# Chunk 0's second row loads through SyncE's queue behind a hold, the weights wait for it, and one key product moves to VectorE

## The chip, the cores and the metric

The kernel runs on one core of a Trainium2 chip. The core has five engines that take their instructions in order, each from its own list: TensorE (PE, matrix products; its loads of stationary operands are shown as PEld), VectorE (DVE), ScalarE (ACT), GpSimd (POOL) and SyncE (SP, which here only issues transfers). Sixteen DMA engines move data between the chip's memory and the core's on-chip memory; a transfer is issued by an engine, POOL or SP for nearly all of them, and lands later. The metric is the device time of one execution in microseconds, as the median of several runs.

## The reference: a gated linear recurrence, then a bilinear feed-forward layer

For 4 batches, 8 heads, 768 tokens and head size 48, the first part keeps a state of 48x48 per batch and head. Each token scales the state's rows by its own alpha, adds the outer product of its key and value, and reads the state with its query:

```python
for t in range(S):
    state = alpha[:, :, t, :, None] * state + np.einsum('bhd,bhe->bhde', k[:, :, t], v[:, :, t])
    y[:, :, t] = np.einsum('bhd,bhde->bhe', q[:, :, t], state)
```

The second part takes all 3072 tokens with their 8x48=384 numbers as x, and gives `(x @ w_a) * (x @ w_b) @ w_out`, with w_a and w_b of 384x1536 and w_out of 1536x384. All inputs and the output are float32.

## The kernel before: six chunks, and a program written out by hand

The work is cut into six chunks, 0 to 5. A chunk holds 256 tokens of two batches; chunks 0 and 1 are the first 256 tokens of batches 0-1 and 2-3, chunks 2 and 3 the next 256, and so on. The two batches of a chunk are its rows, 0 and 1 (in the program, a first argument 0 or 1; `a` and `b` behind it are the two halves of the heads, and `*` is both rows). Two neighbouring tokens share one of the 128 partitions, so a tile of q, k or alpha is 128 x 2 rows x 8 heads x 2 tokens x 48.

A chunk runs through these steps. `ld` loads alpha, q, k or v. `ln` takes the logarithm of alpha on ScalarE. `B`/`Bs` (chunk 0) or `H`, `L`, `A2` (chunk 1) make the running sums of the logarithms over the tokens with a triangular matrix on TensorE, and `E` takes the exponential of a sum or of its negative. `lv` first brings the first of two neighbouring tokens to the level of the second: keys times alpha, queries times the exponential of minus the logarithm (`level`, one multiplication in place on the tile of k or q). `mk` and `mq` multiply keys and queries by the exponentials and write them as bf16 into QKp (`mul`). `C` transposes QKp on TensorE, `Ce` copies the result; `K` and `k` make the new state; `D` makes the scores, `M` or `Mc` with `Mm` mask them; `SB`, `SA` and `Y` add up the outputs, and `X` copies them into xT. The feed-forward part then works on pieces of 128 of the 1536 columns: `a` and `b` are the products with w_a and w_b, `as` copies one of them, `pr` multiplies the two, `o` is the product with w_out, `ot` copies it out and `st` stores it.

The order is written out in the string PROGRAM: each line names a chunk and its steps, and every step appends its instructions to the lists of its engines at once. A step's last letter gives the engine where there is a choice: V for VectorE, P for GpSimd, S for ScalarE, Y for SyncE. So the order of PROGRAM is the order on each engine, and nothing reorders it later. Waits between engines are put in by the framework, from which tile an instruction reads or overwrites. Tiles of alpha, q and k have two buffers each, so chunk 2's alpha goes into chunk 0's buffer and chunk 3's into chunk 1's, and such a load waits for the last instruction that reads the old contents. Loads on POOL's queue also wait so that at most eight are under way.

Around the change: chunk 0's row 0 is loaded in six pieces by SP (`ld a 0b Y` and the like); row 1's alpha, q and k, v, all weights (`W`, `Wo`, which also turn them from float32 into bf16) and chunk 1's loads are issued by POOL. `W b 0 256` loads columns 0 to 255 of w_b. Between its issues POOL builds the constants: `cs` and `cz` clear tiles, `cm` builds half a mask, `c2` and `c3` convert the triangular matrix. A step `gate` exists: POOL copies one element of a tile into a small tile `go`, and so waits until it is there; before the change it is used once in another form (`gatet`), late in the kernel. For row 1 of chunk 1, `lv 1 k P` and `lv 1 q P` stand on POOL with `ld a * P` of chunk 3 between them, and `lv 0 k V` of row 0 on VectorE.

Lines: the loads are line 411, the weights 391, the logarithms 418, `Bs` 465, `lv` 524, `mk` and `mq` 550, `Ce` 599 (VectorE), the transposes 591, the state update 660 and 661, the masks 677 and 685, `pr` 798, the products with w_a and w_b 784 and with w_out 806, and the copy of a gate 858.

Of the kernel before, what the change touches and what calls it, by code (L numbers as in the profile page):

```python
# [14 lines left out]


PROGRAM = """
0: c1a; c1; fill 7 2; cz 0 q V; cz 0 b P; cs 0 m P; ci; cz 1 q V; cz 0 v V; ld a 0b Y; ln 0b; cs 0 0 P; cm 0; cu; cu2 P; B 0b 3; Bs 0b; cs 1 m P; ld v 0 P; ld a 1 P
0: cz 1 b P; ld a 0a Y; ln 0a; B 0a 1; Bs 0a; E 0a b; fill 9 2; cus; ld q 0a Y; mq 0a V; E 0b i; ld q 0b Y; ld k 0a Y; ld k 0b Y; mk 0b V; E 0b b; mq 0b V
0: C 0 1 5; E 0a i; mk 0a V; Ce 0 1 V; C 0 0 3; Ce 0 0 V; dk 0 6; fill 1 1; v 0 S; de 0; K 0 0 7; k 0 0 V; ln 1; cs 1 0 P; ld q 1 P; ld k 1 P; W b 0 256  # L20
0: cm 1; ld v 1 P; c2 P; c3 P; D 0 1 5; M 0 1; D 0 0 0; SB 0 6; B 1a 4; Bs 1a; Mc 0 0; Mm 0 0 V; B 1b 5; Bs 1b; E 1a i; E 1a b; mq 1a V; mk 1a V; K 0 1 4; E 1b i
0: v 1 V; mk 1b V; E 1b b; mq 1b V; SA 0; Y 0; X 0 S; dk 1 0; C 1 0 3; Ce 1 0 V; k 0 1 V; b 1 0 6; W a 0 256; de 1; K 1 0 5; k 1 0 V
1: ld a 1 P
0: W a 256 768; W b 256 768
# [35 lines left out]
0: b 0 1 6  # L60
1: Ce 0 1 S
2: ld k * P
1: lv 1 k P
3: ld a * P
0: pr 0 1
1: mk 1 V; lv 1 q P; mq 1 V
# [202 lines left out]
def kernel(  # L269
# [11 lines left out]
    nc = tc.nc  # L281
    B, H, S, D = q.shape
    assert (B, H, S, D) == (4, 8, 768, 48)
    C = 128
# [14 lines left out]
    ld = ctx.enter_context(tc.tile_pool(name="ld", bufs=2))  # L299
# [89 lines left out]
    def load_w(w, lo, hi):  # L389
        src, dst = ((moe_w_a, wa_t), (moe_w_b, wb_t))[w]  # L390
        nc.gpsimd.dma_start(out=dst[:, :, lo:hi], in_=src[:, lo:hi].rearrange("(t p) f -> p t f", p=128))  # L391

    def load_o(lo, hi):
        nc.gpsimd.dma_start(out=wo_t[:, lo:hi, :], in_=moe_w_out[lo * 128:hi * 128, :].rearrange("(k p) f -> p k f", p=128))
# [11 lines left out]
    def load(ch, what, us, eng):  # L406
        if not hasattr(ch, what):
            setattr(ch, what, ld.tile([C, 2, H, 2, D], BF16 if what == "v" else F32, name=what + "_t", bufs=3 if what == "v" else 2))
        t, src = getattr(ch, what), {"a": alpha, "k": k, "q": q, "v": v}[what]
        us, hs = us  # L410
        eng.dma_start(out=t[:, us, hs].rearrange("p b h r d -> p (b h) (r d)"),  # L411
                      in_=src[ch.b0 + us.start:ch.b0 + us.stop, hs, ch.s * 2 * C:(ch.s + 1) * 2 * C, :].rearrange("b h (p r) d -> p (b h) (r d)", r=2))

    def logs(ch, us):
        if not hasattr(ch, "la"):
            ch.la = wk.tile([C, 2, H, 2, D], F32, name="la", bufs=1)
        us, hs = us
        nc.scalar.activation(out=ch.la[:, us, hs].rearrange("p b h r d -> p (b h r d)"), in_=ch.a[:, us, hs].rearrange("p b h r d -> p (b h r d)"), func=AF.Ln)  # L418

    def pairs(ch, us, eng):  # L420
        if not hasattr(ch, "l2"):
            ch.l2 = wk.tile([C, 3, H, D], F32, name="l2", bufs=1)
        us, hs = us
        ch.apart -= set(range(us.start, us.stop))
        x = ch.la[:, us, hs].rearrange("p b h r d -> p (b h) r d")
        eng.tensor_add(ch.l2[:, us, hs].rearrange("p b h d -> p (b h) d"), x[:, :, 0, :], x[:, :, 1, :])
# [419 lines left out]
    def us(u):  # L846
        return ALL if u == "*" else ONE[int(u)]

    def uh(u):
        return us(u[0]), slice(0, H) if len(u) == 1 else slice(0, H // 2) if u[1] == "a" else slice(H // 2, H)  # L850
# [5 lines left out]
    def gate_t(x, u):  # L856
# [17 lines left out]
        "fill": lambda x, n, i: fill(int(n), i),  # L874
        "warm": lambda x, n, i: warm(int(n), i),
        "ld": lambda x, what, u, e: load(x, what, uh(u), ENG[e]),
        "W": lambda x, w, lo, hi: load_w("ab".index(w), int(lo), int(hi)),
        "Wo": lambda x, lo, hi: load_o(int(lo), int(hi)),
        "ln": lambda x, u: logs(x, uh(u)),
        "l2": lambda x, u, e: pairs(x, uh(u), ENG[e]),  # L880
        "A": lambda x, u, i: cum(x, uh(u), i),
# [81 lines left out]
```

## Time and profile before

| | us |
|---|---|
| median of 3 runs | 194.72 (194.59 to 195.71) |
| the profiled execution | 195.32 |
| its span, first to last instruction | 193.5 |
| PE busy | 184.7 (95% of the span) |
| DVE busy | 138.4 (71%) |
| ACT busy | 103.3 (53%) |
| POOL busy | 50.8 (26%) |
| granted clock of TensorE | 1.00 |

The profile is of one execution. Busy times are of instructions that compute; issuing a transfer is shown with its own rows, and the time from an issue to its landing apart from it. A wait names the engine or transfer whose end came last. In rows of the timeline the first number is the start in us from the span's start and the second the length; where several instructions are merged, xN is their count, and [x <- y] is the idle time ahead of it and what ended it. The 16 DMA engines can have several packets under way, so their share can be above 1.

### The profile page before, as it was taken

To read this page: it belongs to the slowest core of one execution; us is meant where nothing else is said; L and a number is where in the kernel's file an instruction comes from. 1 tells how busy PE (TensorE), PEld (TensorE's weight loads), DVE (VectorE), ACT (ScalarE), POOL (GpSimd) and SP (SyncE) were. 2 spreads that over 40 slices of the span, in tenths; PEclk is the share of its full clock that TensorE was granted. 3 is DMA by queue.
4 is the path that set the end of the run, shared out by engine and by line. 5 is a ranking of instruction groups with operands and counts; after the bars stand their busy time and mean duration, and the time that the engine had idled before them with its cause. 6 is when DMAs were issued, how large, how long until landed. Compare 5 with 4: busy or idle time off the path is not lost.

```text
span 193.5 us, 5877 instructions
## 1 busy us (share of the span) xinstructions
PE 184.7 (95%) x2509; PEld 111.4 (58%) x2509; DVE 138.4 (71%) x230; ACT 103.3 (53%) x189; POOL 50.8 (26%) x71
## 2 busy tenths in 40 slices
PE   7889699999999998999999999999999999999993
PEld 3467475666687865744556644555544566544462
DVE  4688777999899799597979499875854871156520
ACT  4565575886775676556565235875255622154401
POOL 8999645850640425000400020050000000000000
PEclk9999999999999999999999999999999999999999
DMA  5999999999999999489995488999297005021013
GB/s 139 261 214 211 243 247 251 252 246 260 243 220 231 198 234 219 57 233 213 172 219 69 100 203 178 118 191 120 59 180 160 3 3 122 0 99 67 0 42 122
DMA packets 67162, 30.96 MB, mean 160 GB/s; under 512 B 58064, under 2 KB 65120, under 8 KB 67136
## 3 DMA queue, kind: packets, MB, share of 16 engines
q0 software_dynamic: 18640, 14.16, 41.3%
q1 hardware_dynamic: 48352, 16.34, 39.9%
q8 instruction: 19, 0.31, 0.7%
q10 hardware_dynamic: 144, 0.10, 0.2%
q14 instruction: 7, 0.06, 0.1%
HBM read 25.98 MB, written 4.74 MB: 159 GB/s over the span
## 4 chain that ended last, share of the span: by engine, by line
PE 84%; POOL 6%; DMA 5%; issue 2%; DVE 1%; ACT 0%; POOLq 0%; DVEq 0%
PE psum L784 47%; PE psum L806 24%; DMA wb_t<-in_moe_w_b_dram 5%; PE psum L672 3%; PE psum L722 2%; PE psum L625 2%; PE psum L696 2%; PE psum L701 1%; PE psum L505 1%; PE psum L817 1%; POOL v_t L411 1%; POOL a_t L411 1%; PE psum L591 1%; POOL wa_t L391 1%; DVE prod L798 1%
## 5 line engine op out<-in xcount | busy, mean ns | idle before, releaser
L784 PE MATMUL psum<-xT,wb_t 128*128 128x512 bf16 (+1 forms) x270 | 57.0, 337 | 1.3 <-DMA wb_t<-in_moe_w_b_dram 1.3
L784 PE MATMUL psum<-xT,wa_t 128*128 128x512 bf16 (+1 forms) x270 | 56.1, 337 | 0.0
L806 PE MATMUL psum<-wo_t,prod 128*128 128x384 bf16 x276 | 48.5, 326 | 0.0
L784 PEld LDWEIGHTS <-wb_t 128*128 128x128 bf16 x270 | 25.5, 98 | 21.9 <-DMA wb_t<-in_moe_w_b_dram 1.6
L784 PEld LDWEIGHTS <-wa_t 128*128 128x128 bf16 x270 | 25.6, 98 | 19.7 <-issue 0.2
L806 PEld LDWEIGHTS <-prod 128*128 128x128 bf16 x276 | 26.1, 98 | 17.0
L681 ACT ACTIVATE m<-psum 128x1024 bf16<-128x1024 f32 x16 | 16.3, 1023 | 6.1 <-PE psum L672 5.9
L823 DVE COPY ot<-psum 128x384 f32<-128x384 f32 (+1 forms) x13 | 6.9, 538 | 15.7 <-PE psum L806 13.2
L524 POOL TENSOR_TENSOR q_t<-q_t,ra 128x384 f32<-128x384 f32 x8 | 8.8, 1103 | 34.7 <-DVE prod L798 18.4
L821 ACT ACTIVATE ot<-psum 128x384 f32<-128x384 f32 (+1 forms) x12 | 5.7, 477 | 12.9 <-PE psum L806 11.9
L524 POOL TENSOR_TENSOR k_t<-k_t,a_t 128x384 f32<-128x384 f32 x5 | 6.0, 1197 | 22.8 <-DVE QKp L550 17.9
L685 DVE TENSOR_TENSOR m<-m,mask 128x1024 bf16<-128x1024 bf16 x16 | 11.6, 734 | 0.3 <-ACT m L681 0.2
L418 ACT ACTIVATE la<-a_t 128x1536 f32<-128x1536 f32 (+2 forms) x9 | 9.5, 1053 | 3.7 <-DMA a_t<-in_alpha_dram 3.7
L550 DVE TENSOR_TENSOR QKp<-k_t,invb 128x768 bf16<-128x768 f32 x10 | 11.0, 1105 | 0.2
L677 DVE TENSOR_TENSOR m<-psum,mask 128x1024 bf16<-128x1024 f32 x8 | 9.8, 1219 | 1.6 <-PE psum L672 1.5
L550 DVE TENSOR_TENSOR QKp<-q_t,beta 128x768 bf16<-128x768 f32 x10 | 9.3, 947 | 0.0
L672 PE MATMUL psum<-kqT 64*64 64x128 bf16 x384 | 8.6, 218 | 0.2 <-DVE kqT L599 0.2
L411 POOL DMA_DIRECT2D v_t<-in_v_dram x8 | 8.6, 1075 | 0.6 <-PE psum L784 0.5
L762 ACT ACTIVATE ys<-psum 128x768 bf16<-128x768 f32 x7 | 5.6, 808 | 5.6 <-PE psum L722 3.3
L672 PEld LDWEIGHTS <-kqT 64*64 64x64 bf16 x384 | 6.3, 107 | 2.7 <-issue 2.3
L411 POOL DMA_DIRECT2D a_t<-in_alpha_dram x6 | 6.3, 1043 | 5.6 <-DVE prod L798 2.9
L444 PE MATMUL psum<-wz 128*128 128x512 bf16 x17 | 5.5, 473 | 1.2 <-DVE og L336 1.2
(272 smaller groups left out, 272.0 us busy)
## 6 DMA issues: line engine op xcount, KB each, us to landing
out_dram<-ot SPq DMA_DIRECT2D x23, 192.0 KB, 2.6
a_t<-in_alpha_dram POOLq DMA_DIRECT2D x3, 768.0 KB, 14.2
k_t<-in_k_dram SPq DMA_DIRECT2D x3, 768.0 KB, 6.7
q_t<-in_q_dram POOLq DMA_DIRECT2D x2, 768.0 KB, 12.8
v_t<-in_v_dram POOLq DMA_DIRECT2D x4, 384.0 KB, 9.2
q_t<-in_q_dram SPq DMA_DIRECT2D x2, 768.0 KB, 6.7
a_t<-in_alpha_dram POOLq DMA_DIRECT2D x3, 384.0 KB, 5.7
q_t<-in_q_dram POOLq DMA_DIRECT2D x3, 384.0 KB, 13.1
```

What stands on the lines that cost most here:

```text
L411: eng.dma_start(out=t[:, us, hs].rearrange("p b h r d -> p (b h) (r d)"), in_=src[ch.b0 + us.start:ch.b0 + us.stop, hs, ch.s * 2 * C:(ch.s ...
L418: nc.scalar.activation(out=ch.la[:, us, hs].rearrange("p b h r d -> p (b h r d)"), in_=ch.a[:, us, hs].rearrange("p b h r d -> p (b h r d) ...
L524: eng.tensor_mul(x, x, by)
L550: eng.tensor_mul(QKp[ch.c % 2][:, u, j, :, hs, :D], src[:, u, hs].rearrange("p h r d -> p r h d"), f)
L672: nc.tensor.matmul(s2[g * HC:(g + 1) * HC, r, p, rk, :], lhsT=ch.kqT[u][rs, 1, rk, 2 * h + p, g * HC:(g + 1) * HC], rhs=queriesT(ch, u, 2 ...
L677: nc.vector.tensor_mul(m.rearrange("p r a k s -> p (r a) (k s)"), ch.s2[u, h].rearrange("p r a k s -> p (r a) (k s)"), maskn(4))
L681: nc.scalar.activation(out=m.rearrange("p r a k s -> p (r a) (k s)"), in_=ch.s2[u, h].rearrange("p r a k s -> p (r a) (k s)"), func=AF.Copy)
L685: eng.tensor_mul(x, x, maskn(4))
L784: nc.tensor.matmul(p, lhsT=(wa_t, wb_t)[w][:, kk, f * 128:(f + 1) * 128], rhs=ch.xT[:, us.start // 2:us.stop // 2, kk].rearrange("p u g s ...
L806: nc.tensor.matmul(op, lhsT=ch.prod[:, f, at:at + C], rhs=wo_t[:, f, :], start=(f == 0), stop=(f == NFF - 1))
L821: nc.scalar.activation(out=o_, in_=i_, func=AF.Copy)
L823: eng.tensor_copy(o_, i_)
```

## The change

Three things change in PROGRAM, and one step is new.

- `ld a 1`, `ld q 1` and `ld k 1` of chunk 0 (384 KB each) are issued by SP instead of POOL, behind row 0's six loads. Ahead of them a new step `hold a 1` has VectorE clear one element of row 1's alpha tile, right behind the second `Bs`. The alpha load overwrites that element, so it waits for VectorE, and the other two stand behind it in SP's list.
- `gate a 1` on POOL now stands ahead of `W b 0 256`, and `cm 1`, `c2` and `c3` come ahead of the gate. So the weight loads, and everything else on POOL's list behind them, wait until row 1's alpha has landed. `ld v 1` comes behind `W b 0 256`; before, the second mask half stood between the two.
- `lv 1 k` of chunk 1 is done by VectorE instead of POOL. In VectorE's list it stands behind row 1's state update and ahead of `pr 0 1`. POOL's list loses it; what followed it there, chunk 3's alpha load and then `lv 1 q`, stays in this order.

The lists of PE and ACT are the same before and after.

```diff
--- before
+++ after
@@ -15,10 +15,10 @@
 
 
 PROGRAM = """
-0: c1a; c1; fill 7 2; cz 0 q V; cz 0 b P; cs 0 m P; ci; cz 1 q V; cz 0 v V; ld a 0b Y; ln 0b; cs 0 0 P; cm 0; cu; cu2 P; B 0b 3; Bs 0b; cs 1 m P; ld v 0 P; ld a 1 P
-0: cz 1 b P; ld a 0a Y; ln 0a; B 0a 1; Bs 0a; E 0a b; fill 9 2; cus; ld q 0a Y; mq 0a V; E 0b i; ld q 0b Y; ld k 0a Y; ld k 0b Y; mk 0b V; E 0b b; mq 0b V
-0: C 0 1 5; E 0a i; mk 0a V; Ce 0 1 V; C 0 0 3; Ce 0 0 V; dk 0 6; fill 1 1; v 0 S; de 0; K 0 0 7; k 0 0 V; ln 1; cs 1 0 P; ld q 1 P; ld k 1 P; W b 0 256
-0: cm 1; ld v 1 P; c2 P; c3 P; D 0 1 5; M 0 1; D 0 0 0; SB 0 6; B 1a 4; Bs 1a; Mc 0 0; Mm 0 0 V; B 1b 5; Bs 1b; E 1a i; E 1a b; mq 1a V; mk 1a V; K 0 1 4; E 1b i
+0: c1a; c1; fill 7 2; cz 0 q V; cz 0 b P; cs 0 m P; ci; cz 1 q V; cz 0 v V; ld a 0b Y; ln 0b; cs 0 0 P; cm 0; cu; cu2 P; B 0b 3; Bs 0b; cs 1 m P; ld v 0 P
+0: cz 1 b P; ld a 0a Y; ln 0a; B 0a 1; Bs 0a; hold a 1; E 0a b; fill 9 2; cus; ld q 0a Y; mq 0a V; E 0b i; ld q 0b Y; ld k 0a Y; ld k 0b Y; ld a 1 Y; ld q 1 Y; ld k 1 Y; mk 0b V; E 0b b; mq 0b V
+0: C 0 1 5; E 0a i; mk 0a V; Ce 0 1 V; C 0 0 3; Ce 0 0 V; dk 0 6; fill 1 1; v 0 S; de 0; K 0 0 7; k 0 0 V; ln 1; cs 1 0 P; cm 1; c2 P; c3 P; gate a 1; W b 0 256; ld v 1 P
+0: D 0 1 5; M 0 1; D 0 0 0; SB 0 6; B 1a 4; Bs 1a; Mc 0 0; Mm 0 0 V; B 1b 5; Bs 1b; E 1a i; E 1a b; mq 1a V; mk 1a V; K 0 1 4; E 1b i
 0: v 1 V; mk 1b V; E 1b b; mq 1b V; SA 0; Y 0; X 0 S; dk 1 0; C 1 0 3; Ce 1 0 V; k 0 1 V; b 1 0 6; W a 0 256; de 1; K 1 0 5; k 1 0 V
 1: ld a 1 P
 0: W a 256 768; W b 256 768
@@ -60,7 +60,7 @@
 0: b 0 1 6
 1: Ce 0 1 S
 2: ld k * P
-1: lv 1 k P
+1: lv 1 k V
 3: ld a * P
 0: pr 0 1
 1: mk 1 V; lv 1 q P; mq 1 V
@@ -411,6 +411,9 @@
         eng.dma_start(out=t[:, us, hs].rearrange("p b h r d -> p (b h) (r d)"),
                       in_=src[ch.b0 + us.start:ch.b0 + us.stop, hs, ch.s * 2 * C:(ch.s + 1) * 2 * C, :].rearrange("b h (p r) d -> p (b h) (r d)", r=2))
 
+    def hold(ch, what, us):
+        nc.vector.memset(getattr(ch, what)[0:1, us[0], 0, 0, 0:1], 0.0)
+
     def logs(ch, us):
         if not hasattr(ch, "la"):
             ch.la = wk.tile([C, 2, H, 2, D], F32, name="la", bufs=1)
@@ -876,6 +879,7 @@
         "ld": lambda x, what, u, e: load(x, what, uh(u), ENG[e]),
         "W": lambda x, w, lo, hi: load_w("ab".index(w), int(lo), int(hi)),
         "Wo": lambda x, lo, hi: load_o(int(lo), int(hi)),
+        "hold": lambda x, what, u: hold(x, what, uh(u)),
         "ln": lambda x, u: logs(x, uh(u)),
         "l2": lambda x, u, e: pairs(x, uh(u), ENG[e]),
         "A": lambda x, u, i: cum(x, uh(u), i),
```

## The prediction, made before the changed kernel ran

> **What bounds the kernel now.** I read the page's busy times first, then who TensorE waited for, then the chain that ended last in order of time.
>
> ```profile
> PE 184.7 (95%) x2509; PEld 111.4 (58%) x2509; DVE 138.4 (71%) x230; ACT 103.3 (53%) x189; POOL 50.8 (26%) x71
> ...
> PE 84%; POOL 6%; DMA 5%; issue 2%; DVE 1%; ACT 0%; POOLq 0%; DVEq 0%
> ```
>
> TensorE (PE) is busy for 184.7 of 193.5 us and holds 84% of the chain. A change can gain only where PE stands idle, and costs wherever it makes PE idle. The view of the waits has PE's idle times, us in total first:
>
> ```profile
> PE psum L784 <- DMA wb_t<-in_moe_w_b_dram: 1.3, 1, 1.3
> PE psum L701 <- issue: 1.3, 1, 1.3
> ```
>
> Two waits of 1.3 us are the large ones. The chain (start, length, what) tells where the first one lies and what the middle of the kernel looks like:
>
> ```profile
> 14.38 8.97 DMA wb_t<-in_moe_w_b_dram
> ...
> 23.40 0.83 PE psum L784 x6
> ...
> 42.34 0.89 PE psum L591 x16
> 43.23 1.95 PE psum L806 x12
> 45.18 0.80 PE psum L696 x48
> ```
>
> Up to 14.38 us the chain is GpSimd (POOL) issuing loads; then it is the transfer of columns 256 to 768 of w_b, and PE starts at 23.40 when that lands. From 42.34 on each PE piece begins where the last one ended (42.34+0.89=43.23, 43.23+1.95=45.18): nothing there absorbs a delay. So the first part of the change acts ahead of a PE wait of 1.3 us, the last part inside a stretch without slack.
>
> The sum below is made against the profiled execution: 195.32 us, of which 193.5 is the span and 1.82 lies around it. It stands 0.60 above the median of 194.72; I carry the sum over to the median.
>
> **Part 1: three loads leave POOL for SyncE (SP), behind a hold.** The timeline of the start (start, length, engine, line):
>
> ```profile
> 1.09 0.06 DVE L336 MEMSET og<- 128x2 f32 x1
> ...
> 5.23 0.90 POOL L411 DMA_DIRECT2D a_t<-in_alpha_dram  x1
> ...
> 6.03 0.37 DVE L465 TENSOR_TENSOR psum<-psum,la 128x192 f32<-128x192 f32 x1 [0.46 <-PE psum L460]
> ...
> 6.60 0.89 POOL L411 DMA_DIRECT2D q_t<-in_q_dram  x1
> ...
> 7.48 0.89 POOL L411 DMA_DIRECT2D k_t<-in_k_dram  x1
> ...
> 8.02 0.56 DVE L550 TENSOR_TENSOR QKp<-k_t,prod 128x384 bf16<-128x384 f32 x1 [0.51 <-DMA k_t<-in_k_dram]
> ...
> 8.35 0.77 POOL L391 DMA_DIRECT2D wb_t<-in_moe_w_b_dram  x1
> ...
> 10.56 0.90 POOL L411 DMA_DIRECT2D v_t<-in_v_dram  x1
> ...
> 11.14 0.84 ACT L418 ACTIVATE la<-a_t 128x768 f32<-128x768 f32 x1
> ...
> 11.99 0.76 POOL L391 DMA_DIRECT2D wa_t<-in_moe_w_a_dram  x1
> ...
> 14.38 0.76 POOL L391 DMA_DIRECT2D wb_t<-in_moe_w_b_dram  x1
> ...
> 16.20 0.36 DVE L616 COPY vx<-v_t 128x768 bf16<-128x768 bf16 x1 [0.70 <-DMA v_t<-in_v_dram]
> ```
>
> The loads of alpha, q and k of row 1 cost POOL 0.90+0.89+0.89=2.68 us of issuing, the first at 5.23. In the changed kernel the hold, a memset of one element, stands behind VectorE's (DVE) second subtraction, so it runs at 6.03+0.37=6.40. The nearest row for it is the memset of 128x2 at 0.06 us, and DVE idled 0.51 before the product at 8.02, which hides it; uncovered it costs 0.06. SP's queue then holds nothing but these loads behind row 0's six, and what comes next on SP is first used tens of us later. So alpha is issued at about 6.5, 1.3 later than before.
>
> Does the hold free row 0's loads from company? These are the windows (PE, PEld, DVE, ACT, POOL busy, clock, share of the DMA engines, GB/s) and two rows of issues (KB each, median us to landing):
>
> ```profile
> 4.00:6.00 2.00, 1.99 (x11) 1.44 (x11) 0.37 (x1) 0.58 (x2) 2.00 (x3) 1.00 1.08 265
> 6.00:8.00 2.00, 1.86 (x9) 0.66 (x7) 0.98 (x3) 1.57 (x4) 2.00 (x5) 1.00 1.53 194
> 8.00:10.00 2.00, 1.22 (x16) 0.88 (x16) 1.96 (x4) 0.91 (x2) 1.85 (x4) 1.00 1.11 305
> ```
>
> ```profile
> a_t<-in_alpha_dram POOLq DMA_DIRECT2D x3, 384.0 KB, 5.7
> ...
> a_t<-in_alpha_dram SPq DMA_DIRECT2D x1, 768.0 KB, 5.3
> ```
>
> The DMA engines are saturated throughout: 1.08, 1.53 and 1.11 of their time in flight, with 265 GB/s while SP's row-0 loads dominate and 305 while POOL's do. Which queue asks changes the rate little, so the same bytes take about the same time. Row 0's gain is bounded: the whole wait for k, 0.51 us, at best, nothing at worst. Either way PE would only reach its wait for w_b earlier, since that wait ends by a landing. I take 0.
>
> When does row 1's alpha land now? The 768 KB load through SP took 5.3 us; half the bytes at 265 GB/s are 1.5 us fewer, so 3.8 (an estimate from these two rows). That gives 6.5+3.8=10.3, with 6.5+5.3=11.8 as the upper end and 6.5+1.5=8.0 (data alone) as the lower. Before, the logarithm at 11.14 found it landed without a wait; 10.3 leaves that as it is.
>
> **Part 2: the gate.** POOL copies one element of alpha and so waits for it; behind it queue every weight load, v of row 1 and chunk 1's loads. The price of the copy is bounded by 0 and the only such row:
>
> ```profile
> 126.44 0.18 POOL L858 CAST go<-kqT 1x1 f32<-1x1 bf16 x1 [10.91 <-DMA kqT<-QKp]
> ```
>
> I take 0.18. The mask half and the two conversions now stand ahead of the gate, under its wait, so they cost nothing; they were done by 11.99 before and are early now. Gate done at 10.3+0.18=10.5; then w_b's first 256 columns (0.77), v (0.90), then from w_a's first to w_b's second piece as before, 14.38-11.99=2.39: w_b 256 to 768 is issued at 10.5+0.77+0.90+2.39=14.6 against 14.38. The 2.68 us of issuing that POOL saved are spent waiting. v leaves at 11.3 instead of 10.56; DVE got it at 16.20 and would get it up to 0.7 later, which the 1.3 us of PE's wait cover; without them it costs 0.7. The piece of w_b had 8.97 us in a saturated queue behind the same bytes as now, so its landing stays near 23.4. Bounds: at best PE's whole wait goes, -1.3; at worst alpha lands at 11.8, POOL comes 1.5 later, +1.5. I take 0, nearest to the unchanged byte count.
>
> The Trainium skill speaks against the move itself: "DMA: Bandwidth & Descriptors", section "Issuing engines are not separate DMA queues", has all DMAs on the same 16 engines and lets another issuing engine save only the time of initiating. By it part 1 is worth 2.68 us of POOL at most, none of PE. The rates 265 and 305 agree; no row of before shows the three loads on SP.
>
> **Part 3: row 1's key product of chunk 1 goes from POOL to DVE.** The timeline around it, then the same pattern one chunk later:
>
> ```profile
> 33.26 1.33 POOL L524 TENSOR_TENSOR q_t<-q_t,ra 128x384 f32<-128x384 f32 x1
> ...
> 33.84 1.57 DVE L550 TENSOR_TENSOR QKp<-k_t,invb 128x768 bf16<-128x768 f32 x1
> ...
> 36.63 1.01 POOL L524 TENSOR_TENSOR k_t<-k_t,a_t 128x384 f32<-128x384 f32 x1
> ...
> 38.16 1.19 POOL L411 DMA_DIRECT2D a_t<-in_alpha_dram  x1 [0.52 <-POOL k_t L524]
> ...
> 38.93 0.55 DVE L661 TENSOR_TENSOR S<-tmp,bl 128x192 bf16<-128x192 f32 x1
> ...
> 39.38 1.01 POOL L524 TENSOR_TENSOR q_t<-q_t,ra 128x384 f32<-128x384 f32 x1
> 39.40 0.43 DVE L798 TENSOR_TENSOR prod<-as__750,psum 128x256 bf16<-128x256 bf16 x1
> ...
> 39.73 1.48 DVE L550 TENSOR_TENSOR QKp<-k_t,invb 128x768 bf16<-128x768 f32 x1
> ...
> 41.14 0.95 DVE L550 TENSOR_TENSOR QKp<-q_t,beta 128x768 bf16<-128x768 f32 x1
> ...
> 44.35 0.68 DVE L685 TENSOR_TENSOR m<-m,mask 128x1024 bf16<-128x1024 bf16 x1
> ...
> 54.54 0.55 DVE L524 TENSOR_TENSOR k_t<-k_t,a_t 128x384 f32<-128x384 f32 x1
> ...
> 55.83 1.19 POOL L411 DMA_DIRECT2D a_t<-in_alpha_dram  x1 [2.89 <-DVE prod L798]
> ```
>
> POOL did the product at 36.63 to 37.64, long before DVE multiplied the keys at 39.73: hidden. POOL then issued chunk 3's alpha (38.16, 1.19), which overwrites the buffer that the product reads, and then made the query product (39.38 to 40.39) that DVE needs for the multiplication at 41.14. The order on POOL stays: alpha load, then query product. But the load now waits for DVE, where the key product stands behind the state update of 38.93.
>
> Step by step: DVE's key product starts where the product of 39.40 did and takes 0.55 (the row of 54.54 has the same shape on DVE): until 39.95. From such a product to the alpha load that waits for it passed 55.83-(54.54+0.55)=0.74; after POOL's own product it was 38.16-37.64=0.52. Bounds 0 and 0.74; I take 0.74, the same pair of engines. Load at 40.69, done 41.88, query product done 42.89. DVE's query multiplication thus starts at 42.9 instead of 41.14: 1.76 later (DVE itself would be free earlier). The handover from POOL to DVE has no row; 0 to 0.5, I take 0. PE's transposes at 42.34 need the queries, and then masks and scores follow in DVE's order up to the mask product of 44.35, which ended at 45.03, 0.15 ahead of PE's use at 45.18. So PE loses 1.76-0.15=1.6. With no lag it is 0.9; with 0.74 and a handover of 0.5, 2.1.
>
> Is it given back? PE's other wait, 1.3 in the line L701, hangs on the state product of a later chunk, whose work starts after PE's own; it moves along. If it swallowed all it could, 0.3 would be left.
>
> One thing could pay for this. The key multiplications took 1.57 and 1.48 us with a product of POOL's beside them, the query multiplication at 41.14 only 0.95, with POOL issuing a load. In the changed kernel no product runs beside the second of them: 1.48-0.95=0.53 less, against 0.55 more for the product itself. DVE would then be free for the queries at 41.2 as before; what is late is POOL. That is the third rival. The Trainium skill, "SBUF — State Buffer", section "Who interferes with whom", says that a VectorE instruction with two SBUF inputs and a GpSimd instruction that reads SBUF shut each other out for a whole instruction; by that rule the 0.53 is sure and moving the product is free for DVE, and the rows of 1.57 and 1.48 agree with it.
>
> **Sum:** 0 (hold, loads) + 0 (gate, weights) + 1.6 (late query product): 195.32+1.6=196.9, and by the median 194.72+1.6=**196.3 us**.
>
> **The rivals.** (a) *Not slower:* both queues together bring the w_b piece sooner. For it: 305 against 265 GB/s says that the engines have headroom, and the wait at 23.40 is DMA. Against it: the same bytes lie ahead, and POOL reaches the issue no earlier. It decides once the piece lands by 22.1; it takes 1.3 off. With the query product's lag at its lower end (+0.9) the result is 194.72-0.4=194.3, with the lag taken above 195.0. (b) *Much slower:* alpha lands at 11.8, the gate holds POOL, and the w_b piece is 1.5 late: 194.72+1.5+1.6=197.8. For it: POOL's issuing stood on the chain up to 14.38. Against it: the queue is full, so a late issue need not be a late landing. (c) *The product is free:* DVE's key multiplication is 0.53 shorter, and the query product's delay is partly hidden or given back at L701: +0.3, 195.0. For it: the two long rows. Against it: POOL's order, alpha before query. That the hold doesn't do what it says (row 0's loads share the engines only with v anyway) is part of the forecast: it changes nothing.
>
> **How the numbers follow.** Forecast 0.58 (195.6 to 196.8), (a) 0.16 (194.3 to 195.0, a small part lower), (b) 0.13, (c) 0.13. The range 194.4 to 197.2 takes in the forecast with both ends of its lags, (c) and most of (a); left out are (b) and the rest of (a), under 0.2. One per cent, about what a measurement of this kernel can tell from no change, is 192.8 and 196.7. Slower by more: (b) and three tenths of the forecast, 0.30. Faster by more: 0.04, (a) with no late product at all. The rest, 0.66, lies within.
>
> **What would show it.** Alpha of row 1 on SP's queue at 6.5 and w_b's second piece at 14 to 15 on POOL, PE's wait for it ending at 23 to 24: parts 1 and 2 right. POOL's load of chunk 3's alpha at 40 to 41 (released by DVE) and its query product at 41.5 to 42.5, PE idle before the transposes near 42 for over 1 us: part 3 right. The forecast is wrong if PE's wait for w_b is gone or over 2 us, or if no PE idle time appears near 42.

## The result and the profile after

The changed kernel takes 198.25 us (197.33 to 198.57, four runs) against 194.87 for the kernel before beside it: 1.0151 times as long, 95% interval 1.0119 to 1.0184, so about 2.9 us slower (2.3 to 3.6); the two medians lie 3.4 apart. Ratios here leave out executions more than 1.5% above the fastest of the same kernel. The profiled execution, 198.57, is the slowest of the four; its span of 196.8 is 3.3 more than the span of before. The prediction said 196.3, 1.6 slower, with a range to 197.2: right in sign, about half in size, and outside the range. The two rows of the page that answer to those shown of before, in the changed kernel (lines below 411 are as before, those behind the new function are 3 higher):

```profile
PE 186.8 (95%) x2509; PEld 112.8 (57%) x2509; DVE 139.1 (71%) x232; ACT 103.3 (52%) x189; POOL 47.8 (24%) x68
...
PE 76%; POOL 8%; DMA 6%; issue 4%; DVE 3%; ACT 0%; POOLq 0%; DVEq 0%
```

TensorE's share of the chain fell from 84 to 76%. Its waits, us in total, times, longest:

```profile
PE psum L594 <- DVE QKp L553: 1.4, 3, 0.7
PE psum L628 <- DVE vx L619: 1.2, 2, 0.9
...
PE psum L787 <- DMA wb_t<-in_moe_w_b_dram: 0.6, 1, 0.6
```

The start of the changed kernel in the timeline, then its windows (the last two numbers of a row are the share of the DMA engines and GB/s):

```profile
7.26 0.37 DVE L468 TENSOR_TENSOR psum<-psum,la 128x192 f32<-128x192 f32 x1 [0.90 <-PE psum L463]
...
7.61 0.06 DVE L415 MEMSET a_t<- 1x1 f32 x1
...
7.70 0.37 SPq L411 DMA_DIRECT2D a_t<-in_alpha_dram  x1
...
11.48 0.18 POOL L857 COPY go<-a_t 1x1 f32<-1x1 f32 x1 [3.71 <-DMA a_t<-in_alpha_dram]
...
11.95 0.78 POOL L391 DMA_DIRECT2D wb_t<-in_moe_w_b_dram  x1 [0.29 <-issue]
...
12.73 0.90 POOL L411 DMA_DIRECT2D v_t<-in_v_dram  x1
...
16.01 0.77 POOL L391 DMA_DIRECT2D wb_t<-in_moe_w_b_dram  x1
...
17.98 0.62 DVE L619 COPY vx<-v_t 128x768 bf16<-128x768 bf16 x1 [1.85 <-DMA v_t<-in_v_dram]
...
24.78 0.83 PE L787 MATMUL psum<-xT,wb_t 128*128 128x256 bf16 x6 [0.64 <-DMA wb_t<-in_moe_w_b_dram]
```

```profile
6.00:8.00 2.00, 2.00 (x9) 1.31 (x9) 0.89 (x4) 0.34 (x1) 1.50 (x6) 1.00 1.48 213
8.00:10.00 2.00, 1.75 (x14) 0.74 (x11) 1.82 (x4) 2.00 (x5) 0.00 (x0) 1.00 0.70 135
10.00:12.00 2.00, 1.93 (x60) 1.45 (x60) 1.53 (x3) 0.69 (x4) 0.23 (x2) 1.00 1.20 289
```

The hold ran at 7.61 instead of the 6.40 that I had worked out, SyncE issued alpha at 7.70, and GpSimd stood idle 3.71 us at the gate until it landed. Between 8 and 10 us the DMA engines were in use for 0.70 of their time and moved 135 GB/s, where before it was 1.11 and 305: row 0's loads had ended, row 1's had hardly begun, and no weight load was allowed. The late piece of w_b left at 16.01 instead of 14.38 and landed at 24.7 instead of 23.4. Row 1's v came late too: VectorE waited 1.85 us for it (0.70 before) and copied it 1.8 us later than before, and TensorE waited 0.86 us for VectorE. So TensorE itself came late to the piece of w_b. These are its rows ahead of the wait, before and after:

```profile
20.51 1.59 PE L784 MATMUL psum<-xT,wa_t 128*128 128x256 bf16 x12
```

```profile
22.55 1.59 PE L787 MATMUL psum<-xT,wa_t 128*128 128x256 bf16 x12
```

Before, it was ready at 20.51+1.59=22.10 and waited 1.30 us; in the changed kernel it was ready at 24.14 and waited 0.64. Had the piece landed at 23.4 as before, TensorE would still have started on it 0.7 later than before. Of the 1.4 us there, the landing adds 0.6 on top of a late v and late sums.

The later stage, where the key product moved (changed kernel):

```profile
34.90 0.88 DVE L527 TENSOR_TENSOR k_t<-k_t,a_t 128x384 f32<-128x384 f32 x1 [0.48 <-DMA k_t<-in_k_dram]
...
39.62 0.44 PE L628 MATMUL psum<-vx,QKp 64*64 64x48 bf16 x32
...
41.24 0.55 DVE L527 TENSOR_TENSOR k_t<-k_t,a_t 128x384 f32<-128x384 f32 x1
...
42.08 1.15 POOL L411 DMA_DIRECT2D a_t<-in_alpha_dram  x1 [3.42 <-DVE k_t L527]
...
43.25 1.01 POOL L527 TENSOR_TENSOR q_t<-q_t,ra 128x384 f32<-128x384 f32 x1
...
44.30 0.96 DVE L553 TENSOR_TENSOR QKp<-q_t,beta 128x768 bf16<-128x768 f32 x1 [1.31 <-POOL q_t L527]
...
45.31 0.84 PE L594 MATMUL psum<-ident,QKp 128*128 128x128 bf16 x12 [0.72 <-DVE QKp L553]
...
47.51 0.69 DVE L688 TENSOR_TENSOR m<-m,mask 128x1024 bf16<-128x1024 bf16 x1
...
48.26 0.86 PE L699 MATMUL psum<-m,vx 64*64 64x128 bf16 x48
```

And the rows of before that answer to the first two:

```profile
33.18 0.56 DVE L524 TENSOR_TENSOR k_t<-k_t,a_t 128x384 f32<-128x384 f32 x1
...
37.59 0.44 PE L625 MATMUL psum<-vx,QKp 64*64 64x48 bf16 x32
```

VectorE's key product, GpSimd's alpha load, its query product and VectorE's query multiplication follow each other with at most 0.3 us between them: 41.24, 42.08, 43.25, 44.30. VectorE waited 1.31 us for GpSimd there, TensorE 0.72 us ahead of its transposes.

Between the two profiles the delay grows like this: 24.78-23.40=1.4 us when TensorE gets w_b's piece; 39.62-37.59=2.0 at the state products of chunk 1, whose keys landed late as well (34.90 instead of 33.18, with a wait); 48.26-45.18=3.1 at the output products behind the late queries. From there it stays about so to the end, 3.3. Two profiles alone do not say what each part costs by itself; that took runs.

### The profile page after: what moved, and what is told of

Same layout as the page of the kernel before. It is cut to its first block, busy times and chain, and to the rows that moved or that the text cites. A ratio compares the mean times of both kernels' runs of the same rounds, so it can differ in the third digit from the quotient of the medians.

```text
span 196.8 us, 5883 instructions
## 1 busy us (share of the span) xinstructions
PE 186.8 (95%) x2509; PEld 112.8 (57%) x2509; DVE 139.1 (71%) x232; ACT 103.3 (52%) x189; POOL 47.8 (24%) x68
## 4 chain that ended last, share of the span: by engine, by line
PE 76%; POOL 8%; DMA 6%; issue 4%; DVE 3%; ACT 0%; POOLq 0%; DVEq 0%
PE psum L787 43%; PE psum L809 21%; DMA wb_t<-in_moe_w_b_dram 4%; PE psum L675 2%; PE psum L725 2%; DMA a_t<-in_alpha_dram 2%; PE psum L699 2%; PE psum L628 2%; PE psum L704 1%; POOL v_t L411 1%; PE psum L508 1%; DVE m L688 1%; POOL q_t L527 1%; POOL a_t L411 1%; PE psum L820 1%
## 5 line engine op out<-in xcount | busy, mean ns | idle before, releaser
L688 DVE TENSOR_TENSOR m<-m,mask 128x1024 bf16<-128x1024 bf16 x16 | 12.8, 811 | 0.3 <-ACT m L684 0.2
L553 DVE TENSOR_TENSOR QKp<-k_t,invb 128x768 bf16<-128x768 f32 x10 | 10.5, 1050 | 0.2
L527 POOL TENSOR_TENSOR k_t<-k_t,a_t 128x384 f32<-128x384 f32 x4 | 5.2, 1319 | 22.2 <-DVE QKp L553 17.5
L411 POOL DMA_DIRECT2D a_t<-in_alpha_dram x5 | 5.3, 1063 | 9.3 <-DVE prod L801 3.9
L628 PEld LDWEIGHTS <-QKp 64*64 64x64 bf16 x320 | 4.8, 108 | 4.4 <-issue 3.7
## 6 DMA issues: line engine op xcount, KB each, us to landing
wo_t<-in_moe_w_out_dram POOLq DMA_DIRECT2D x2, 576.0 KB, 14.8
```

The lines of the kernel that those rows point to most:

```text
L527: eng.tensor_mul(x, x, by)
L553: eng.tensor_mul(QKp[ch.c % 2][:, u, j, :, hs, :D], src[:, u, hs].rearrange("p h r d -> p r h d"), f)
L628: nc.tensor.matmul(kv[r * DP:(r + 1) * DP, e:e + D], lhsT=QKp[ch.c % 2][gs, u, 1, rk, 2 * p + r, :], rhs=value(ch, gs, u, rk, 2 * p + r), ...
L688: eng.tensor_mul(x, x, maskn(4))
```

## Experiments

Three groups: the parts alone, the order of causes at the start, and what can be saved. Ratios are against the kernel before in the same series, with their 95% intervals; 1% is 1.95 us. The edits are shown by the steps that change; the rest of each line of PROGRAM is left out.

**The key product alone** (the kernel before, with this one edit):

```diff
-1: lv 1 k P
+1: lv 1 k V
```

> Only the key product moves to VectorE; loads, weights and GpSimd's order at the start are those of before. Theory A (late query product: GpSimd's alpha load waits for the product, and the query product stands behind that load): 1.0 to 1.6 us slower than before, and TensorE idle for 0.6 to 1.2 us ahead of the transposes near 42 to 44 us, waiting for VectorE's query multiplication. Theory B (the loads and the gate make the whole loss, the product is hidden): within 0.3 us of before and no such idle time.

Measured: 1.0099 (1.0069 to 1.0130), 1.9 us slower. Its timeline:

```profile
36.96 0.44 PE L625 MATMUL psum<-vx,QKp 64*64 64x48 bf16 x32
...
38.57 0.55 DVE L524 TENSOR_TENSOR k_t<-k_t,a_t 128x384 f32<-128x384 f32 x1
...
39.64 1.15 POOL L411 DMA_DIRECT2D a_t<-in_alpha_dram  x1 [3.64 <-DVE prod L798]
...
40.81 1.00 POOL L524 TENSOR_TENSOR q_t<-q_t,ra 128x384 f32<-128x384 f32 x1
...
41.84 0.96 DVE L550 TENSOR_TENSOR QKp<-q_t,beta 128x768 bf16<-128x768 f32 x1 [1.52 <-POOL q_t L524]
...
45.80 0.87 PE L696 MATMUL psum<-m,vx 64*64 64x128 bf16 x48
```

VectorE's product ends at 38.57+0.55=39.12, the alpha load starts at 39.64, the query product follows it, and VectorE waits 1.52 us. Theory A holds, at or a little above the upper end of its size; theory B, that the product is hidden, falls. From TensorE's state products to its output products, the first and the last row here, passed 45.80-36.96=8.84 us, against 45.18-37.59=7.59 before and 48.26-39.62=8.64 in the changed kernel: this step costs 1.25 and 1.05 us in the traces. The profiled execution, 195.80, was the fastest of its ten; what the others lost beyond this step is not shown.

**The same with GpSimd's two steps turned round** (against the kernel before):

```diff
-1: lv 1 k P
-3: ld a * P
+1: lv 1 k V
...
-1: mk 1 V; lv 1 q P; mq 1 V
+1: mk 1 V; lv 1 q P; mq 1 V
+3: ld a * P
```

> Start of before; key product on VectorE as in the changed kernel, but on GpSimd the query product comes ahead of chunk 3's alpha load. Theory A (the loss of the product alone is the alpha load standing ahead of the query product): the query multiplication follows the key multiplication without a wait and the loss of 1.0% goes: within 0.5 us of before. Rival G (the 0.55 us more on VectorE make the loss): 1 us or more slower, as the product alone.

Measured: 1.0003 (0.9972 to 1.0033). The multiplications follow each other:

```profile
40.76 0.95 DVE L550 TENSOR_TENSOR QKp<-k_t,invb 128x768 bf16<-128x768 f32 x1
...
41.62 0.95 DVE L550 TENSOR_TENSOR QKp<-q_t,beta 128x768 bf16<-128x768 f32 x1
```

The whole loss of the part goes with the order on GpSimd, and the 0.55 us more on VectorE cost nothing that shows: rival G falls. Moving work off GpSimd lost time only because a load that waited for the moved work stood ahead of the next product.

**The loads, hold and gate alone** (the changed kernel with `lv 1 k P`):

```diff
-1: lv 1 k V
+1: lv 1 k P
```

> Hold, gate and loads through SyncE as in the changed kernel, the key product back on GpSimd. Theory A (two costs that add): 1.4 to 2.2 us slower than before; VectorE's query multiplication of chunk 1 follows its key multiplication with no wait. Theory B: 3 us or more slower. Theory C (the loss at the start is the slow matrix products of the running sums, a matter of the clock and not of the change): with the second subtraction at 6.0 us instead of 7.3 the loss is 0.5 us or less.

Measured: 1.0115 (1.0060 to 1.0171), 2.2 us slower. The hold was late here too, at 7.52. VectorE's query multiplication had no wait. The size is theory A's. The two parts by themselves make 4.1 us against 2.9 for the whole; with these intervals that is no contradiction, but that they simply add is not shown. In this trace TensorE waited for pieces of w_a, 0.30 and 0.75 us, and then hardly at all for w_b's piece, which it started on at 24.80: the weights came late as a whole, not this piece alone. Theory C was not put to the test here, since the sums ran slow again.

**The changed kernel with the query product first** (the same turn of GpSimd's two steps):

```diff
-3: ld a * P
 ...
 1: mk 1 V; lv 1 q P; mq 1 V
+3: ld a * P
```

> The changed kernel with the query product ahead of chunk 3's alpha load on GpSimd. Theory A (costs add): 1.0 to 1.6 us faster than the changed kernel, so 1.4 to 2.4 us slower than before, and no wait of VectorE's query multiplication for GpSimd. Rival I (the loss of the loads hides the product): as slow as the changed kernel, 3 us.

Measured: 1.0074 (1.0044 to 1.0105), 1.4 us slower than before. Against the 1.0151 of the changed kernel, in another series, 1.5 us came back. Rival I falls. So within the changed kernel the split is about 1.5 for the late query product and 1.4 for the loads (2.2 in the run before, the intervals overlap).

**Without the hold** (loads alone, the gate stays):

```diff
-hold a 1;
```

> As the run with the loads alone, but without the hold: row 1's loads stand behind row 0's in SyncE's queue and are issued at once, about 4 us, the gate stays. Theory A (the gap in the transfers behind the hold makes the loss): alpha lands by 9.5, the gate opens by 9.7 and the late piece of w_b is issued by 14; no window from 4 to 12 us has the DMA share under 0.9; within 0.5 us of before. Rival D (SyncE's queue or the gate costs by itself): 1.4 us or more slower, as with the hold.

Measured: 1.0044 (1.0009 to 1.0080), 0.9 us slower. This lies between theory A's half microsecond and rival D's 1.4, and alpha's landing was a miss: issued at 4.00, it opened the gate only at 10.95, not by 9.7. Issuing it earlier did not bring it earlier: before, it was issued at 5.23 and landed 5.1 us later, at 10.3. The window of 8 to 10 us had a share of 1.36, so the gap was gone, and that alpha shared the engines with row 0's loads is the likely reason. The hold does keep these apart: row 0's v, issued at about 4.2 in every kernel, landed 4.6 us later before, 4.5 with the early hold below, and 6.1 to 7.0 in the four kernels without a hold whose row-1 loads go through SyncE. TensorE waited 0.5 and 0.4 us for its copy in two of them.

**The gate alone** (the kernel before, with the order of the changed one on GpSimd, row 1's loads staying there):

```diff
-W b 0 256
-0: cm 1; ld v 1 P; c2 P; c3 P; D 0 1 5
+cm 1; c2 P; c3 P; gate a 1; W b 0 256; ld v 1 P
+0: D 0 1 5
```

> Only the gate and the order of constants and weights of the changed kernel; row 1's loads stay on GpSimd's queue, the product stays there too. Theory A (a gate costs what GpSimd's issues come later, by itself): gate at 10.4 to 10.8, late piece of w_b issued at about 15 instead of 14.4, 0.3 to 1.0 us slower. Rival H (the loads on SyncE's queue make the loss that stayed without the hold): within 0.3 us of before.

Measured: 1.0028 (0.9993 to 1.0062), 0.5 us slower, with the gate's copy at 10.56 and the piece of w_b issued at 14.73. The gate found alpha landed and did not wait; what came later is the order of constants and weights. (In this trace the granted clock of TensorE was 0.50 from 11.2 to 14.4 us, so its matrix products are not compared with those of before.) Theory A's size, but the interval reaches just past no change: a cost of the gate by itself is likely and not shown.

**The hold at two other places** (loads alone). Behind row 0's last key multiplication, with the three loads behind it:

```diff
-Bs 0a; hold a 1; E 0a b
+Bs 0a; E 0a b
...
-ld a 1 Y; ld q 1 Y; ld k 1 Y; mk 0b V
+mk 0b V
...
-mk 0a V; Ce 0 1 V
+mk 0a V; hold a 1; ld a 1 Y; ld q 1 Y; ld k 1 Y; Ce 0 1 V
```

> Loads alone as before (product on GpSimd), with the hold about 2.5 us later, behind row 0's last key multiplication. Theory A (the hold's time sets alpha's landing, the gate and the weights one for one): alpha issued at 9.6 to 10.2, gate at 13.5, late piece of w_b issued at 18 and landing at 26 to 27, 4 to 5 us slower than before, a window of 8 to 12 us with the DMA share under 0.5. Rival E (the transfers are bound by bytes, order matters little): no more than 0.5 us slower than with the hold at its place.

Measured: 1.0199 (1.0145 to 1.0253), 3.9 us slower, a little under theory A's 4 to 5. Its window of 8 to 10 us and its gate:

```profile
8.00:10.00 2.00, 1.52 (x17) 0.82 (x16) 1.90 (x6) 1.41 (x3) 0.16 (x1) 1.00 0.07 6
...
13.49 0.18 POOL L857 COPY go<-a_t 1x1 f32<-1x1 f32 x1 [5.33 <-DMA a_t<-in_alpha_dram]
```

The engines are all but empty for two microseconds, and gate, w_b's piece and its landing come at the times that theory A gave. Rival E falls: the bytes do not set the landing once the queue has run dry. In this trace the granted clock was 0.50 from 15.8 to 25.8 us, so TensorE's times in it are not used; the clock does not make the loss, since two runs at a mean clock of 0.999 took 199.14 and 199.90. Likewise the one run of the changed kernel at 1.00 was its slowest. And one instruction earlier, behind the first subtraction:

```diff
-B 0b 3; Bs 0b; cs 1 m P
+B 0b 3; Bs 0b; hold a 1; cs 1 m P
...
-Bs 0a; hold a 1; E 0a b
+Bs 0a; E 0a b
```

> Loads alone (product on GpSimd), the hold one instruction earlier, behind the first subtraction of the running sums instead of the second: alpha issued at 5.4 to 6.1. Theory A (alpha's issue sets gate and weights): gate at about 10.4 to 10.9, between the run without a hold and the run with the hold at its place: 0.5 to 1.0% slower than before, no window of 8 to 10 us under a DMA share of 0.9. Rival C (the slow running sums make the loss, not the hold): as slow as with the hold at its place wherever the second subtraction is late.

Measured: 1.0108 (1.0041 to 1.0176), 2.1 us slower with a wide interval; the window of 8 to 10 us had a share of 1.18. The trace is as theory A has it, the time is at or a little above its upper end and does not separate the early hold from the one in its place. All of them in a table; times in us, the landing being the issue plus what the trace gives from there:

| run | alpha issued | gate | w_b's piece issued | landed | ratio |
|---|---|---|---|---|---|
| before | 5.23 | none | 14.38 | 23.4 | 1 |
| no hold | 4.00 | 10.95 | 15.12 | 23.9 | 1.0044 |
| gate alone | 5.23 | 10.56 | 14.73 | 22.9 | 1.0028 |
| hold early | 5.94 | 10.34 | 14.86 | 23.2 | 1.0108 |
| loads alone | 7.60 | 11.46 | 15.98 | 24.8 | 1.0115 |
| hold late | 9.63 | 13.49 | 17.99 | 26.7 | 1.0199 |

From 7.6 on the later hold moves alpha's issue, the gate, the piece's issue and its landing by about 2 us each, and the kernel by 1.6. With alpha issued before 6 the landing stays between 22.9 and 23.9, and the ratios, 1.0028 to 1.0108, cannot be told apart. The landing scatters by itself: with row 1's loads and the weights in the place of before it came at 22.6, 23.0, 23.4 and 23.6 in four traces; with the hold at its place at 24.7, 24.8 and 25.2 in three. So the table ties the loss to the hold firmly only at its late end.

**No hold and no gate** (loads through SyncE, product on GpSimd):

```diff
-hold a 1;
-gate a 1;
```

> Row 1's loads through SyncE's queue without hold and without gate: GpSimd issues the weights as soon as it gets there, the late piece of w_b about 11.5 us. Theory E (the bytes ahead set the landing): the piece lands at 23 to 24 as before, within 0.5 us of before. Rival F (GpSimd's issuing set it): the piece lands by 22 and TensorE's wait for it is gone, 1 us or more faster.

Four runs, one of 193.5 and three of 196.43, 196.63 and 196.79: with two such groups no interval is given. The piece of w_b was issued at 11.73 and landed at 22.2, 2.7 and 1.2 us earlier than before, and TensorE's wait for it was gone. So rival F is half right and theory E wrong: GpSimd's issuing does move the landing, by under half of what it gains (21.9, 21.9 and 22.2 in the three traces without hold and gate, against 22.6 to 23.6 with the loads of before). But the kernel was not reliably faster; at the transposes near 37 us TensorE waited 0.8 us for VectorE.

**The running sums made slow.** In the changed kernel and some others the matrix products of the running sums took longer. Rows of before, then of the changed kernel (the fillers ahead, the eight sums, the fillers behind):

```profile
1.20 2.99 PE L444 MATMUL psum<-wz 128*128 128x512 bf16 x7 [1.20 <-DVE og L336]
...
4.20 1.72 PE L460 MATMUL psum<-la,ut 128*128 128x192 f32 x8
...
5.76 2.11 PE L444 MATMUL psum<-wz 128*128 128x512 bf16 x9
```

```profile
1.20 3.17 PE L447 MATMUL psum<-wz 128*128 128x512 bf16 x7 [1.20 <-DVE og L336]
...
4.26 2.89 PE L463 MATMUL psum<-la,ut 128*128 128x192 f32 x8
...
6.95 2.14 PE L447 MATMUL psum<-wz 128*128 128x512 bf16 x9
```

Fillers of one size take 3.17/7=0.45 us at first and 2.14/9=0.24 later, so TensorE works at about half its speed and then at full; in the profile of before the change came ahead of the sums, in the changed kernel at about their end. The second subtraction, which follows the sums, began at 5.9 to 6.0 in three kernels, 6.3 to 6.5 in five and 7.1 to 7.3 in four, all with the same fillers. The profile's row of the granted clock shows 1.00 throughout in both, so it does not tell this. The Trainium skill, "TensorE: Matmul & The Clock Gate", "Part 1: The HAM clock gate", says that the clock rises after a busy window of about 3.4 us which runs freely and does not start with the kernel; the scatter agrees, though no run here sets the window, and in before the speed had risen by 4.20, only 3.0 us after the first filler at 1.20. To take the chance out, six of the seven fillers ahead were dropped from the kernel before:

```diff
-fill 7 2; cz 0 q V
+fill 1 2; cz 0 q V
```

> The kernel before with one instead of seven filling matrix products ahead of the running sums, so that the sums run slow every time (second subtraction at 7.0 to 7.4). Theory A (without the hold, slow sums only shorten TensorE's wait for w_b, and the transfers don't move): the late piece of w_b issued at 14.4 and landing at 23.4 as before, within 0.5 us of before. Rival C (slow sums cost by themselves): 1.0 us or more slower.

Measured: 1.0013 (0.9978 to 1.0049). The sums were slow as meant:

```profile
7.17 0.37 DVE L465 TENSOR_TENSOR psum<-psum,la 128x192 f32<-128x192 f32 x1 [0.91 <-PE psum L460]
```

The nine fillers behind them stayed slow too (3.82 us instead of 2.11). The piece of w_b was issued at 14.8 and landed at 23.0, and TensorE started on it at 23.25 without a wait: the slow start had used up the 1.3 us of slack. So slow sums cost nothing that shows in the kernel before: theory A, rival C falls. The hold hangs the transfers on them: it ran about 0.35 us behind the start of the second subtraction in all three traces with the hold at its place (7.61, 7.52, 7.42). No trace with this hold and fast sums was caught, so how much of the loads' loss would stay with fast sums is open. The same edit without hold and gate (loads through SyncE, product on GpSimd):

```diff
-hold a 1;
-gate a 1;
-fill 7 2; cz 0 q V
+fill 1 2; cz 0 q V
```

> No hold and no gate, loads through SyncE, and the sums made slow in the same way. If the two groups of times of the run without hold and gate (193.5 and 196.5) are fast and slow sums, nothing covers the slow ones there, since TensorE does not wait for w_b: all runs near 196.5, none near 193.5. If not, both groups come again.

Measured: 1.0101 (1.0038 to 1.0165), all four runs from 196.15 to 198.62, none near 193.5. This agrees with fast sums in the single run of 193.5 above, and the traced execution of that kernel, 196.79, had slow ones, but no trace of the 193.5 exists, so it is not shown. The trace shows where the earlier weights were lost:

```profile
34.70 2.44 DVE L553 TENSOR_TENSOR QKp<-q_t,beta 128x768 bf16<-128x768 f32 x1
...
37.19 0.40 PE L594 MATMUL psum<-ident,QKp 128*128 128x128 bf16 x4 [1.43 <-DVE QKp L553]
```

VectorE's query multiplication of chunk 1's row 0 took 2.44 us instead of 0.95, and TensorE waited 1.43 for it.

**What is left of the change without its waits**: no hold, no gate, the product on VectorE, the query product first (the changed kernel with the edits above).

```diff
-hold a 1;
-gate a 1;
-3: ld a * P
 ...
 1: mk 1 V; lv 1 q P; mq 1 V
+3: ld a * P
```

> Loads through SyncE without hold and gate, the key product on VectorE, and the query product ahead of chunk 3's alpha load: what the other runs leave of the change once its waits are taken out. If the run without hold and gate lost its gain to GpSimd's key product beside VectorE's query multiplication (1.75 to 2.44 us long there instead of 0.95, TensorE waiting 0.8 to 1.4 us near 37 us), this product is now elsewhere: the multiplication is back at 0.95, the transposes wait under 0.5 us, and the kernel is 0.5 to 1.5 us faster than before. If something else holds TensorE there (the landings of chunk 1's keys and queries), it is within 0.5 us of before or slower.

Measured over five rounds: 0.9995 (0.9965 to 1.0025). The multiplication was back at 0.94 and the transposes waited 0.47, as expected of the first case, yet the time is that of before. TensorE started on w_b's piece at 22.57 instead of 23.40, but came to the same output products as in the row of 45.18 only at 44.9: the 0.8 us gained at w_b had shrunk to 0.3 by then. Which wait would have to go next wasn't tried.

## Why the prediction was wrong, step by step

**Right.** The late query product: its mechanism, its order (product, alpha load, query product, multiplication) and roughly its size, 1.6 forecast against 1.9 (1.3 to 2.5) alone and 1.5 within the changed kernel. That 1.6 lies so near is in part luck: the lag from VectorE's product to the alpha load was 42.08-41.79=0.29 and, alone, 0.52, not 0.74. With these the same sum gives 1.15 and 1.4, and the traces show 1.05 and 1.25 at this step. The handover from GpSimd to VectorE was 0.04, as taken. Alpha's way through SyncE's queue: 11.35-7.70=3.65 us from issue to landing against 3.8. GpSimd's work behind the gate: 16.01-11.95=4.06, as worked out. That the move of the loads by itself brings nothing: alpha issued at 4.00 landed no earlier than the one issued at 5.23 before, and the kernel with the free loads took the time of before.

**The step that failed** is the end of part 2: "I take 0, nearest to the unchanged byte count". The piece of w_b landed 1.4 us late, and the loads alone cost 1.4 to 2.2. Under it lay two wrong readings. First, "The DMA engines are saturated throughout" was read from before, where GpSimd kept feeding them from 5.23 on. The hold and the gate take this feed away: the share fell to 0.70 between 8 and 10 us, and to 0.07 with a late hold. A full queue in the trace of before is no evidence for a kernel that stops filling it. Second, the hold's time of 6.40 came from one profile; it was 7.61, since the sums ran slow. Alpha then landed at 11.35, near the upper end of 11.8 that I had worked out and set aside, and another 0.29 us passed from the gate to the next issue. The row to distrust was the one with the 9 fillers at 0.23 us each behind 7 at 0.43: it shows that the speed changed just ahead of the sums.

A second term at nothing was row 1's v: "up to 0.7 later, which the 1.3 us of PE's wait cover". It came 17.98-16.20=1.8 later and TensorE waited 0.86 for it; with the late sums, TensorE was ready for the piece only at 24.14. So even a landing at 23.4 would not have made this part 0. And the remark that what the hold does for row 0's loads changes nothing overlooked row 0's v, which landed 1.5 us or more later in the kernels without a hold.

Rival (b), 0.13, had this mechanism and 197.8 as its price: that is what happened, by a wait of GpSimd at the gate and a late piece, with TensorE itself late besides. Rival (a) failed for the change as it is; without hold and gate the landing did come 1.2 us earlier, and the gain was lost later. Rival (c): the multiplication was indeed back at 0.95, and it did not help, since the queries were late. The line that I thought might give something back, L701 (L704 in the changed kernel), waited 0.9 instead of 1.3.

## What to carry to other kernels

A wait put into a queue of transfers can let the queue run empty, and whatever the wait hangs on (here matrix products whose speed differed from trace to trace) is then in the path of all that stands behind it. A slack read from a profile, such as the 1.3 us at w_b, covers only one delay: ask of every engine that ends there how late it may come. Before moving work off an engine, look at what comes next there: a load that overwrites the moved work's input now waits for the other engine, and everything behind the load with it. If such a move is wanted, put the work that others need ahead of that load; here this alone took the product's loss of 1.0% to nothing that shows.

## What was unexpected of the hardware

TensorE's speed doubled at a different time from kernel to kernel, between about 4 and 7 us with the same instructions ahead, while the profile's clock row stayed at 1.00. Elsewhere that row does move: in three traces (gate alone, hold late, changed kernel with the query product first) it fell to 0.50 for 3 to 10 us, starting 1.4 to 2.4 us behind a stretch of 1 to 2 us in which TensorE was idle (7.8 to 8.8, 12.3 to 14.3 and 17.6 to 18.9 us). In the latter two, three matrix products with a weight piece took 0.80 to 0.85 us there instead of 0.49. The changed kernel's 0.86 us of idle time at 17.8 was not followed by such a fall; what decides it stays open. Alpha issued 1.2 us earlier through the other queue, without a hold, landed no earlier (gate at 10.95; landing at 10.3 before). And VectorE's query multiplication, 0.95 us alone, took 1.75 and 2.44 us in the traces of the two kernels without hold and gate whose key product was on GpSimd; GpSimd issued a load and made a product in that time, but an issue beside the same multiplication in other runs left it at 0.94, and why it is long there stays open.
